# A second fixed order of steps for a pooled-attention and feed-forward kernel, without its twelve filler matmuls

## The chip, the core and the metric

The kernel runs on one core of a Trainium2 chip. The time is device microseconds of one execution; the number compared is the median of the runs of each kernel. TensorE is called PE here, its weight loads PEld, VectorE is DVE, ScalarE is ACT, GpSimd is POOL, and SP issues the DMAs.

## What is computed

Attention over keys and values that are averaged in groups of eight (72 of each are left per head), and behind it a layer norm and a feed-forward block of 512 to 2048 to 512 with a residual, all in float32:

```
k_p = k.reshape(B, H, Sp, pool, D).mean(axis=3)
v_p = v.reshape(B, H, Sp, pool, D).mean(axis=3)
attn = softmax(scale * q @ k_p^T)             # 8 batches x 8 heads, 576 queries, D = 64
x = (attn @ v_p), heads side by side          # 4608 tokens x 512
xn = (x - mu) / np.sqrt(var + 1e-06) * g_ln
out = x + np.maximum(xn @ w_ch1, 0.0) @ w_ch2 # 512 -> 2048 -> 512
```

## The kernel before

Tokens go through in 36 tiles of 128, and the feed-forward block in nine chunks of 512 tokens. Every wide product is made of three f16 matmuls (high times high, low times high, high times low), so each operand has to be split in a high and a low half first; the weights are converted and split on the chip as well.

Each stage is a Python generator whose `yield`s cut it into steps: a step issues instructions to one or two engines. The names that the text uses:

- A.t, the scores of token tile t (eight matmuls, L788; the maximum and subtraction are DVE L798 and L803), and B.t, its values: matmuls L923 to L928, DVE L935 to L956 (row sums, division into tile x, norm statistics), and for the first tiles `parts_turned`, which transposes x on PE with four matmuls into f32 (L876) and one more (L884). B.2 means token tile 2, V.10 is token tile 10 (DVE L982 to L1014).
- C, the conversion of a block of weights (DVE L540); M1 and M2, the maxima that give the scales (ending in a transposition on PE, L467, after DVE L577 to L445); S, the split of a block (ACT L480, DVE L487).
- F.c.f, for chunks 0 and 1, one tile of 128 hidden units of chunk c: twelve matmuls L1111, then ACT L1120 and DVE L1122 out of the PSUM pool ps_f. F.0.f.0 and F.0.f.1 for the first few f are the two halves of the columns.
- G.c.t.h, for chunks 0 to 2, one output tile of 128 tokens and half of the hidden units: 24 matmuls L1314, then DVE L1325 adds to x.
- P.c.h.f.m and O.c.h.n.u, from chunk 2 on, the products of Strassen's scheme in two by two blocks (seven instead of eight): six matmuls L1155 for each product of the first layer, twelve matmuls L1272 for each of the second. ACT L1174 and DVE L1169 and L1172 bring the first ones into a sum in `raw`, DVE L1193 splits them (EL, ER, EP), DVE L1289 adds the second ones to x.
- T, TW: sums of weight blocks that Strassen's scheme needs (T: DVE L615 to L623; TW: DVE L1234 and POOL L1239 to L1247); HK and HV: loads of keys and values and their average (DVE L652, L658; L669); TS.c: a square root by iteration in twelve small DVE instructions (L1029 to L1060); Z and XT: splitting normalised x on POOL and ACT (L1078, L1080) and transposing it by DMA.

What sets the order of the work is written out by hand: two strings of tokens, START (to the end of chunk 1) and STEADY (the rest). Under a manual schedule `run` goes through a string, and each time a token appears it runs the next step of that generator. Every engine so executes its instructions in the order of the strings; semaphores alone decide when.

```
for token in tokens.split():
    if token not in begun:
        name, *args = token.split(".")
        begun[token] = iter(ops[name](*map(int, args)) or ())
    next(begun[token], None)
```

ps_f holds three tiles in START. `KEEP_BUSY = {2: 12}` (L57) makes `parts_turned` issue twelve matmuls of the identity (L872) ahead of its third call (B.2), into the PSUM tile that the transposition then overwrites.

## Time and profile before

| | us |
|---|---|
| runs, shortest, median, longest | 811.84, 813.9, 815.95 |
| the profiled execution, its own time | 814.76 |
| its span in the trace | 813.0 |
| PE busy in the span | 782.8 (96%) |
| DVE busy | 664.0 (82%) |
| ACT, POOL busy | 470.7, 487.6 |

PE is the engine that has least room: 30 us of its span are idle. A span is what lies between the first and the last instruction; 1.8 us lie around it. The median is 0.9 us below the profiled execution.

### The profile page before, as it was taken

The page shows a single profiled execution, that of the slowest core. Times are in us where ns is not written, and L with a number is a line of the kernel's source. Part 1 is how long each engine was busy: PE and PEld are TensorE (multiplying, and loading weights), DVE is VectorE, ACT ScalarE, POOL GpSimd, SP SyncE. Part 2 cuts the span into 40 slices and gives each one's busy share as a digit, 9 for nine tenths or more (in the row PEclk, how much of TensorE's full clock was granted, in tenths as well). Part 3 has the DMA queues.
Part 4 walks back from the last instruction along what each step waited for, and adds up shares of the span by engine and source line. Part 5 has one row for each costly group of instructions (what it writes and reads, how often), then busy time and mean ns, then how long its engine had stood idle before and what let it go on. Part 6 is the DMA issues. An engine that isn't in the chain of part 4 may idle for free.

```text
span 813.0 us, 17388 instructions
## 1 busy us (share of the span) xinstructions
PE 782.8 (96%) x6618; PEld 609.5 (75%) x6618; DVE 664.0 (82%) x1352; ACT 470.7 (58%) x880; POOL 487.6 (60%) x601
## 2 busy tenths in 40 slices
...
DVE  5998999778658999698998998998797868875654
...
GB/s 352 277 151 306 205 188 150 215 8 1 44 120 126 165 217 132 192 188 242 190 174 183 211 192 243 134 250 164 243 85 206 166 134 168 174 152 161 76 120 130
DMA packets 181507, 138.91 MB, mean 171 GB/s; under 512 B 143792, under 2 KB 151600, under 8 KB 179248
## 3 DMA queue, kind: packets, MB, share of 16 engines
...
q14 instruction: 31, 0.25, 0.1%
...
## 4 chain that ended last, share of the span: by engine, by line
PE 54%; DVE 6%; ACT 1%; DMA 1%; issue 1%; DVEq 0%; ACTq 0%
PE ps_f L1155 25%; PE ps_f L1272 25%; PE ps_a L788 2%; PE ps_f L1314 1%; DVE w L1193 1%; DMA ring<-w2s 1%; PE ps_a L927 1%; PE ps_a L928 1%; DVE ring L1185 1%; DVE x L1289 0%; DVE raw L1172 0%; DVE phl L1169 0%; DVE mx L798 0%; DVE raw L1013 0%; DVE raw L1169 0%
## 5 line engine op out<-in xcount | busy, mean ns | idle before, releaser
L1272 PE MATMUL ps_f<-ring,w 128*128 128x256 f16 x2016 | 231.5, 273 | 2.4 <-DVE w L1193 1.0
L1272 PEld LDWEIGHTS <-w 128*128 128x128 f16 x2016 | 196.4, 98 | 26.6 <-DVE w L1193 1.6
L1155 PE MATMUL ps_f<-zts,w 128*128 128x256 f16 x1680 | 206.7, 273 | 2.9 <-DVE raw L1169 1.4
L1155 PEld LDWEIGHTS <-w 128*128 128x128 f16 x1680 | 163.5, 98 | 23.7 <-issue 4.2
L1314 PE MATMUL ps_f<-w,ring 128*128 128x512 f16 x576 | 126.6, 379 | 2.6 <-DVE x L1325 2.2
L1174 ACT COPY raw<-ps_f 128x256 f32<-128x256 f32 x160 | 56.4, 373 | 91.4 <-PE ps_f L1155 80.8
L1314 PEld LDWEIGHTS <-ring 128*128 128x128 f16 x576 | 56.1, 98 | 68.9 <-issue 3.4
L1155 PE MATMUL ps_f<-zts,tsp 128*128 128x256 f16 x672 | 91.0, 273 | 1.7 <-ACT raw L1174 1.7
L1111 PE MATMUL ps_f<-zts,w 128*128 128x512 f16 (+1 forms) x480 | 86.9, 338 | 1.5 <-DVE w L487 1.4
L1191 ACT CAST w<-w 128x512 f16<-128x512 f32 x96 | 58.9, 618 | 44.6 <-POOL w L1211 24.5
L1193 POOL TENSOR_TENSOR w<-w 128x512 f16<-128x512 f32 x48 | 58.3, 1214 | 32.2 <-ACT w L1191 24.4
L1111 PEld LDWEIGHTS <-w 128*128 128x128 f16 x480 | 46.3, 98 | 37.8 <-DVE w L487 1.9
L1155 PEld LDWEIGHTS <-tsp 128*128 128x128 f16 x672 | 65.0, 98 | 10.1 <-issue 2.2
L1210 POOL TENSOR_TENSOR w<-raw 128x256 f32<-128x256 f32 x32 | 25.0, 780 | 65.5 <-ACT raw L1202 37.9
L1289 DVE SCALAR_TENSOR_TENSOR x<-ps_f,y,x 128x256 f32<-128x256 f32 (+1 forms) x84 | 42.0, 517 | 24.2 <-PE ps_f L1272 23.1
L824 POOL TENSOR_TENSOR phl<-e,phl 128x512 f16<-128x512 f32 x32 | 39.0, 1220 | 37.5 <-ACT phl L814 37.5
L1080 POOL TENSOR_TENSOR hl<-raw,hl 128x640 f16<-128x640 f32 x28 | 40.9, 1463 | 25.9 <-ACT hl L1078 25.8
L1289 DVE SCALAR_TENSOR_TENSOR x<-ps_f,cy,x 128x256 f32<-128x256 f32 (+1 forms) x84 | 42.2, 516 | 14.1 <-PE ps_f L1272 13.6
L1193 DVE TENSOR_TENSOR w<-raw,w 128x512 f16<-128x512 f32 (+1 forms) x64 | 45.0, 709 | 3.9 <-ACT w L1191 3.9
L788 PE MATMUL ps_a<-kblk,q 128*128 128x144 f32 (+1 forms) x320 | 43.3, 294 | 3.7 <-issue 2.5
L1169 DVE TENSOR_TENSOR raw<-ps_f,raw 128x256 f32<-128x256 f32 x80 | 32.2, 415 | 15.9 <-ACT raw L1174 9.4
L1120 ACT ACTIVATE ring<-ps_f 128x512 f16<-128x512 f32 (+1 forms) x40 | 19.4, 506 | 43.9 <-PE ps_f L1111 29.6
...
## 6 DMA issues: line engine op xcount, KB each, us to landing
...
```

The source lines that it names most:

```text
L788: nc.tensor.matmul(ps[r, p // 2, p % 2 * 2 * KV : (p % 2 + 1) * 2 * KV], lhsT=q[:, p, r], rhs=kblk[b % NKB][:, p, :], start=True, stop=True,)
L824: nc.gpsimd.tensor_tensor(out=ph[:, 0, :, KA:P], in0=e[:, :, 0:KA], in1=ph[:, 0, :, 0:KA], op=ALU.subtract)
L1080: nc.gpsimd.tensor_tensor(out=zhl[:, 1, :], in0=src, in1=zhl[:, 0, :], op=ALU.subtract)
L1111: nc.tensor.matmul(ps, lhsT=w[:, part, fs], rhs=zT[:, kz, cols], start=(n == 0), stop=(n == 3 * NKT - 1),)
L1155: nc.tensor.matmul(ps, lhsT=w[:, part, f * P : (f + 1) * P], rhs=z, start=m in (1, 2, 4, 5) and n == 0, stop=m in (2, 3, 4, 7) and n == 3 ...
L1169: nc.vector.tensor_tensor(out=o, in0=ps, in1=o, op=ALU.add)
L1174: nc.scalar.copy(out=o, in_=ps)
L1191: nc.scalar.copy(out=hi, in_=src)
L1193: engine.tensor_tensor(out=lo, in0=src, in1=hi, op=ALU.subtract)
L1272: nc.tensor.matmul(ps, lhsT=wt[2][:, left, part, f * HC + u * P : f * HC + (u + 1) * P], rhs=b[:, f // FPB, wp, f % FPB], start=n < 4 and ...
L1289: nc.vector.scalar_tensor_tensor(out=x, in0=ps, scalar=scale, in1=x, op0=ALU.mult, op1=ALU.add)
L1314: nc.tensor.matmul(ps, lhsT=h[:, part, i, cols], rhs=w[:, wp, j], start=(n == 0), stop=(n == 3 * NFT // 2 - 1),)
```

## The change

Both strings are replaced. They hold the same work, in another order on every engine, and the filler matmuls with their counter are gone (24 rows of PE, twelve matmuls and twelve weight loads). The numbers of lines fall by 2 below the strings and by 9 below `parts_turned`: L876 is L867 after, L1111 is L1102, L1325 is L1316, L1193 is L1184.

```
-KEEP_BUSY = {2: 12}
...
 START = """
-LN.2 LN.2 LK.0 LK.0 LK.1 LK.1 Q.0 Q.0 R.1.0 R.1.0 R.1.1 R.1.1 Q.1 Q.1 R.1.2 R.1.2 R.1.3 R.1.3 A.0 HV.1.0 LG LG R.2.0
...
+LN.2 LN.2 LK.0 LK.0 LK.1 LK.1 Q.0 Q.0 LG LG R.1.0 R.1.0 R.1.1 R.1.1 Q.1 Q.1 R.1.2 R.1.2 R.1.3 R.1.3 A.0 HK.1.0 HV.1.0
...
 STEADY = """
-P.2.0.0.2 P.2.0.0.1 P.2.0.0.5 P.2.0.1.2 P.2.0.0.1 P.2.0.0.1 P.2.0.0.6 P.2.0.1.1 P.2.0.1.1 P.2.0.1.1 P.2.0.0.5 P.2.0.0.5
...
-    n_turned = [0]
-
     def parts_turned(x, ln, cv, dst):
         ps = psum["ps_m"].tile([P, CH], F32, name="ps_m").rearrange("p (k c) -> p k c", k=NKT)
-        n_turned[0] += 1
-        for _ in range(KEEP_BUSY.get(n_turned[0] - 1, 0)):
-            nc.tensor.matmul(
-                ps, lhsT=ident, rhs=ident.unsqueeze(1).broadcast_to([P, NKT, P]), start=True, stop=True
-            )
         for k in range(NKT):
```

Three places of the new order are shown. The first is PE just ahead of the transposition of token tile 2 (x). Before, the last two of the twelve fillers (`ident`) stand there:

```order
L872 LDWEIGHTS ident
L872 MATMUL ps_m<-ident 128x512
L876 MATMUL ps_m<-zts,x 128x128 x4
L884 MATMUL ps_m<-zts,ln 128x512
L923 LDWEIGHTS pt
```

After, the last of 36 matmuls of the first layer stand there (F.0.0.0, F.0.1.0 and F.0.2.0, w_90 being the split weights):

```order
L1102 LDWEIGHTS w_90
L1102 MATMUL ps_f<-zts,w_90 128x256
L867 MATMUL ps_m<-zts,x 128x128 x4
L875 MATMUL ps_m<-zts,ln 128x512
L914 LDWEIGHTS pt
```

These 36 stood behind that transposition, and behind the values of tile 3, before.

The second place is DVE at the start of the second half of the first layer of chunk 1 (F.1.8 and on; L1325 is the last addition of G.1.3.0, L1122 takes a tile out of ps_f; raw is a weight sum of T or a normalised tile of V.10, kr keys, or TW where it comes from w_91). Before:

```order
L1325 SCALAR_TENSOR_TENSOR x<-ps_f,cy,x 128x512
L623 TENSOR_TENSOR raw<-raw 128x512
L935 TENSOR_SCALAR sm<-ps_a,cv 128x8
L943 RECIPROCAL rs<-sm 128x8
L945 TENSOR_TENSOR x<-ps_a,rs 128x512
L955 BN_STATS st<-x 128x6
L956 BN_AGGR ln<-st 128x2
L982 TENSOR_SCALAR z<-x,ln 128x512
L1122 SCALAR_TENSOR_TENSOR ring<-ps_f,ring 128x512 x5
L982 TENSOR_SCALAR raw<-x,ln 128x512
L1007 TENSOR_SCALAR raw<-x,ln 128x512
```

After:

```order
L1316 SCALAR_TENSOR_TENSOR x<-ps_f,cy,x 128x512
L621 TENSOR_TENSOR raw<-raw 128x512
L1113 SCALAR_TENSOR_TENSOR ring<-ps_f,ring 128x512
L650 TENSOR_REDUCE kr<-kr 128x72
L656 COPY kblk_114<-kr 64x72 x2
L973 TENSOR_SCALAR raw<-x,ln 128x512
L998 TENSOR_SCALAR raw<-x,ln 128x512
L1225 TENSOR_TENSOR kr<-w_91 128x256 x2
L1002 TENSOR_TENSOR raw<-raw 128x256
L1003 TENSOR_TENSOR raw<-raw 128x256
L1004 TENSOR_TENSOR raw<-raw 128x256
L1005 TENSOR_TENSOR raw<-raw 128x256
```

Before, five ps_f tiles (F.1.8 to F.1.12) were taken out in a row, and the average of keys, V.10 and TW.0.0.0 came later. After, those stand between the first tile and the second.

The third place is DVE between the last sums of the second half of chunk 3's first layer and the second layer that reads them (L1193 writes the split factors w_91, L1169 and L1172 the sums in raw, L1029 and L1032 open TS.4, L976 is a small step of token tile 19). Before:

```order
L1193 TENSOR_TENSOR w_91<-phl_116,w_91 128x256
L669 TENSOR_REDUCE vp<-vr 72x64
L1169 TENSOR_TENSOR raw<-ps_f,raw 128x256 x2
L1193 TENSOR_TENSOR w_91<-w_91 128x2x256
L1172 TENSOR_TENSOR raw<-ps_f,raw 128x2x256
L976 TENSOR_SCALAR ln<-ln 128x1
L1193 TENSOR_TENSOR w_91<-raw,w_91 128x2x256 x2
```

After:

```order
L667 TENSOR_REDUCE vp<-vr 72x64
L1160 TENSOR_TENSOR raw<-ps_f,raw 128x256
L1020 TENSOR_SCALAR ve<-ln 128x4
L1023 TENSOR_SCALAR y<-ve 128x4
L1184 TENSOR_TENSOR w_91<-w_91 128x2x256
L1163 TENSOR_TENSOR raw<-ps_f,raw 128x2x256
L1184 TENSOR_TENSOR w_91<-raw,w_91 128x2x256
L967 TENSOR_SCALAR ln<-ln 128x1
L1184 TENSOR_TENSOR w_91<-phl_116,w_91 128x256
L1184 TENSOR_TENSOR w_91<-raw,w_91 128x2x256
```

The split `w_91<-phl_116` (ER.3.1.1) has moved behind the sum L1172, and TS.4 has come in ahead; the splits EL.3.1.2 and EL.3.1.3 are the rows `w_91<-raw` in both.

On PE around G.2 (chunk 2's second layer, groups of 24 matmuls L1314 among groups of six matmuls L1155) the order after the scores of tile 17 was, before: G.2.0.1, two products, G.2.3.1, two products, G.2.2.1. After: G.2.3.1, G.2.0.1, one product, G.2.2.1, the values of tile 16, one product, G.2.1.1.

## Rows read from the trace of the kernel before

**Rows 1.** The page: the span, busy time of each engine, and the busy tenths of DVE in 40 slices of 20.3 us (9 is 90% or more).

```profile
span 813.0 us, 17388 instructions
PE 782.8 (96%) x6618; PEld 609.5 (75%) x6618; DVE 664.0 (82%) x1352; ACT 470.7 (58%) x880; POOL 487.6 (60%) x601
...
DVE  5998999778658999698998998998797868875654
```

**Rows 2.** Windows of the span: stretch, length, then busy us (and instructions) of each engine, the granted clock as a share of full speed, the DMA share and GB/s.

```profile
100.00:120.00 20.00, 17.38 (x93) 9.27 (x92) 19.38 (x30) 16.96 (x25) 17.23 (x22) 0.91 0.79 195
...
112.00:114.00 2.00, 2.00 (x9) 1.65 (x9) 2.00 (x2) 2.00 (x4) 1.92 (x2) 0.50 0.72 183
...
380.00:400.00 20.00, 20.00 (x196) 18.06 (x195) 18.15 (x36) 16.02 (x33) 12.71 (x13) 1.00 0.77 168
```

**Rows 3.** The waits of PE over the whole span: line, what it waited for, us in total, times, the longest.

```profile
PE ps_m L728 <- DMA w<-in_kvn_dram: 6.8, 1, 6.8
...
PE ps_f L1155 <- DVE raw L1169: 1.4, 2, 0.8
...
PE ps_f L1272 <- DVE w L1193: 1.0, 2, 0.8
```

**Rows 4.** The timeline of PE and, below, of DVE around the fillers: start, length (of the group), engine, line, operation, count, and in brackets the idle time before it and what ended it.

```profile
42.84 2.75 PE L872 MATMUL ps_m<-ident 128*128 128x512 bf16 x12 [0.63 <-ACT z L897]
...
46.82 1.16 PE L876 MATMUL ps_m<-zts,x 128*128 128x128 f32 x8 [1.23 <-DVE x L945]
...
49.45 4.09 PE L1111 MATMUL ps_f<-zts,w 128*128 128x256 f16 x36
...
46.07 0.69 DVE L945 TENSOR_TENSOR x<-ps_a,rs 128x512 f32<-128x512 f32 x1
...
47.63 1.45 DVE L487 SCALAR_TENSOR_TENSOR w<-w,gs 128x1024 f16<-128x1024 f32 x1
```

**Rows 5.** The timeline of PE from 104 to 120 us, where the clock was halved; the last row is DVE's.

```profile
109.96 0.39 PE L1111 MATMUL ps_f<-zts,w 128*128 128x512 f16 x1 [1.44 <-DVE w L487]
...
111.53 2.26 PE L788 MATMUL ps_a<-kblk,q 128*128 128x144 f32 x8 [1.18 <-issue]
...
113.58 3.21 PE L1111 MATMUL ps_f<-zts,w 128*128 128x512 f16 x12
...
117.15 2.75 PE L1111 MATMUL ps_f<-zts,w 128*128 128x512 f16 x12
...
119.74 0.22 PE L467 MATMUL ps_m<-ident,rowmax 128*128 128x128 bf16 x1
...
117.74 0.15 DVE L445 TENSOR_SCALAR rowmax<-rowmax 128x1 int32<-128x1 int32 x1
```

**Rows 6.** The timeline of DVE from 199 to 225 us, the steps that the second place above moves.

```profile
200.90 1.63 DVE L623 TENSOR_TENSOR raw<-raw 128x512 f32<-128x512 f32 x1 [0.72 <-POOL raw L621]
...
207.22 0.69 DVE L1122 SCALAR_TENSOR_TENSOR ring<-ps_f,ring 128x512 f16<-128x512 f32 x1 [1.62 <-ACT ring L1120]
...
212.80 0.54 DVE L982 TENSOR_SCALAR raw<-x,ln 128x512 f32<-128x512 f32 x1
...
213.71 0.42 DVE L1011 TENSOR_TENSOR raw<-raw 128x256 f32<-128x256 f32 x1
...
220.57 0.74 DVE L652 TENSOR_REDUCE kr<-kr 128x72 f32<-128x576 f32 x1
...
221.34 1.05 DVE L658 COPY kblk<-kr 64x72 f32<-64x72 f32 x2
...
222.43 2.83 DVE L1234 TENSOR_TENSOR kr<-w 128x256 f32<-128x256 f16 x2
```

**Rows 7.** The timeline of PE from 255 to 327 us, the groups that waited; the last row is DVE's.

```profile
256.71 0.49 PE L1155 MATMUL ps_f<-zts,tsp 128*128 128x256 f16 x3 [1.08 <-ACT raw L1174]
...
277.55 0.81 PE L1155 MATMUL ps_f<-zts,w 128*128 128x256 f16 x6 [0.58 <-DVE raw L1169]
...
301.91 1.47 PE L1155 MATMUL ps_f<-zts,w 128*128 128x256 f16 x12 [0.37 <-DVE x L1325]
...
304.64 0.81 PE L1155 MATMUL ps_f<-zts,tsp 128*128 128x256 f16 x6 [0.61 <-ACT raw L1174]
...
310.53 1.22 PE L788 MATMUL ps_a<-kblk,q 128*128 128x144 f32 x8 [0.81 <-PE ps_f L1155]
...
326.95 5.34 PE L1314 MATMUL ps_f<-w,ring 128*128 128x512 f16 x24 [2.23 <-DVE x L1325]
...
326.15 0.75 DVE L1325 SCALAR_TENSOR_TENSOR x<-ps_f,cy,x 128x512 f32<-128x512 f32 x1
```

**Rows 8.** The timeline of DVE, and in the last row of PE, from 391 to 401 us, and the opening of TS.4 where it stood.

```profile
391.53 1.09 DVE L1193 TENSOR_TENSOR w<-phl,w 128x256 f16<-128x256 f32 x1
...
393.81 0.67 DVE L1193 TENSOR_TENSOR w<-w 128x512 f16<-128x512 f32 x1
394.40 0.68 DVE L1172 TENSOR_TENSOR raw<-ps_f,raw 128x512 f32<-128x512 f32 x1
...
395.13 1.53 DVE L1193 TENSOR_TENSOR w<-raw,w 128x512 f16<-128x512 f32 x2
...
409.40 0.95 DVE L1029 TENSOR_SCALAR ve<-ln 128x4 f32<-128x4 f32 x1
...
395.74 5.40 PE L1272 MATMUL ps_f<-ring,w 128*128 128x256 f16 x48
```

More of the change, by code (lines that the diff above doesn't have):

```diff
@@ new lines @@
+B.12 P.2.1.1.5 P.2.1.1.5 P.2.1.0.5 P.2.1.0.5 P.2.1.1.6 P.2.1.0.6 P.2.1.0.3 P.2.1.1.3 P.2.1.1.6 P.2.1.1.6 P.2.1.0.6
+P.2.1.0.6 TW.0.2.1 B.13 P.2.1.0.2 P.2.1.0.2 P.2.1.0.4 TW.0.3.0 B.13 TW.0.3.0 TW.0.3.0 P.2.1.0.3 P.2.1.0.3 P.2.1.1.2
+A.15 HV.4.1 HV.4.1 HK.4.0 TW.0.2.1 TW.0.2.1 P.2.1.1.3 P.2.1.1.3 TW.0.3.0 P.2.1.1.2 P.2.1.1.2 P.2.1.1.4 P.2.1.0.7
+P.2.1.1.7 B.12 HV.4.1 HV.4.1 A.15 B.14 G.2.0.0 A.15 P.2.1.0.4 P.2.1.0.4 B.13 HK.4.0 HK.4.0 A.16 TW.0.3.0 TW.0.3.0
+HK.4.1 KW.1.0 KW.1.0 HV.5.0 B.14 HV.4.1 A.15 A.15 A.15 KW.0.1 KW.0.1 B.14 B.14 P.2.1.1.4 P.2.1.1.4 B.13 P.2.1.0.7
@@ new lines @@
+ES.3.0.0 ES.3.0.0 P.3.0.3.1 P.3.0.3.1 P.3.0.3.6 ER.3.0.0 ER.3.0.0 P.3.0.3.5 P.3.0.3.5 EP.3.0.0.1 EP.3.0.0.0 P.3.0.2.1
+P.3.0.2.1 P.3.0.3.3 TW.1.3.1 TW.1.3.1 TW.1.3.1 HV.5.1 LW.3.0.0 LW.3.0.0 A.19 LW.3.0.1 LW.3.0.1 G.2.2.1 G.2.2.1
+P.3.0.1.3 P.3.0.1.3 P.3.0.2.5 EL.3.0.1 P.3.0.3.6 P.3.0.3.6 B.16 P.3.0.3.2 P.3.0.3.2 P.3.0.3.4 P.3.0.3.4 P.3.0.3.4
+EP.3.0.0.1 EP.3.0.0.1 A.18 B.17 P.3.0.2.6 P.3.0.2.2 P.3.0.2.2 P.3.0.2.4 P.3.0.3.7 EP.3.0.0.0 EP.3.0.0.0 P.3.0.3.3
+P.3.0.3.3 P.3.1.0.2 EL.3.0.3 P.3.0.2.4 P.3.0.2.4 P.3.0.2.5 P.3.0.2.5 P.3.0.2.6 P.3.0.2.6 A.18 P.3.0.2.3 P.3.1.0.1
@@ new lines @@
+O.5.1.0.0 O.5.1.0.0 EP.5.1.2.1 EP.5.1.2.1 O.5.1.0.1 O.5.1.0.1 O.5.1.1.1 O.5.1.1.1 O.5.1.2.1 O.5.1.1.0 O.5.1.1.0
+ES.5.1.3 ES.5.1.3 EP.5.1.3.1 O.5.1.3.0 O.5.1.3.0 B.27 B.27 Z.27.0 Z.27.1 TS.6 O.5.1.2.1 O.5.1.2.1 TS.6 Z.27.0 Z.27.0
+EP.5.1.3.1 EP.5.1.3.1 HK.7.0 HK.7.0 LW.5.1.5 LW.5.1.5 LW.5.1.4 LW.5.1.4 A.29 A.29 O.5.1.2.0 O.5.1.4.0 P.6.0.0.1
+O.5.1.5.0 O.5.1.4.1 P.6.0.0.1 P.6.0.0.1 LW.5.1.6 LW.5.1.6 XT.27.0 XT.27.0 HK.7.1 O.5.1.2.0 O.5.1.2.0 Z.27.1 Z.27.1
+XT.27.1 XT.27.1 O.5.1.3.1 O.5.1.3.1 O.5.1.5.1 O.5.1.4.1 O.5.1.4.1 O.5.1.6.1 A.28 A.28 A.28 O.5.1.4.0 O.5.1.4.0
@@ new lines @@
+P.6.1.3.5 P.6.1.2.2 B.30 B.30 Z.30.0 Z.30.1 O.6.0.5.1 O.6.0.5.1 P.6.1.3.1 P.6.1.2.5 O.6.0.5.0 P.6.1.2.5 P.6.1.2.5
+P.6.1.3.1 P.6.1.3.1 EP.6.1.0.0 EP.6.1.0.0 ER.6.1.0 ER.6.1.0 P.6.1.2.2 P.6.1.2.2 P.6.1.2.4 B.31 P.6.1.2.3 P.6.1.2.6
+P.6.1.2.4 P.6.1.2.4 EP.6.1.0.1 P.6.1.3.5 P.6.1.3.5 P.6.1.2.6 P.6.1.2.6 ES.6.1.1 EP.6.1.1.0 EL.6.1.1 EL.6.1.1 Z.30.1
+Z.30.1 O.6.0.5.0 O.6.0.5.0 P.6.1.3.2 P.6.1.3.6 P.6.1.2.7 P.6.1.3.3 P.6.1.3.6 P.6.1.3.6 XT.30.1 XT.30.1 LW.6.1.2
+LW.6.1.2 P.6.1.3.7 EP.6.1.0.1 EP.6.1.0.1 B.31 P.6.1.2.3 P.6.1.2.3 EL.6.1.2 ES.6.1.1 ES.6.1.1 P.6.1.3.2 P.6.1.3.2
```

586 lines of the change are left out of this document (283 added, 303 removed).

## The prediction

> **What bounds the kernel now.** I read the page first: PE is busy for 782.8 of 813.0 us [rows 1], so 30.2 us of its time are idle, and no order of the same work can take more than that away. The first 6.8 us of it wait for a load [rows 3] that the change leaves where it is, and another part is the tail behind PE's last matmul, whose tokens are nearly the same. Some 20 us are left, and the question is which engine ends them. The windows answer that for the first 120 us: DVE is at nine tenths or more in most of these slices [rows 1], and from 100 to 120 it works 19.38 of 20 us while PE works 17.38 [rows 2]. DVE is the bound there, and PE's waits are what DVE's queue leaves. Later PE runs through whole windows without a gap (20.00 of 20 from 380 to 400), with DVE close behind at 18.15 [rows 2]. So only a place where DVE now finishes earlier, or where PE has more to do before it asks DVE, can gain; and where DVE gets more to do ahead of a result, new waits can come.
>
> **The change, part by part.** The sum is made on the profiled execution (span 813.0, time 814.76) and then taken off the median of the runs, 813.9.
>
> 1. *The fillers.* They took 2.75 us, and yet PE waited 1.23 us more behind them, for L945 of token tile 2, which ended at 46.07 + 0.69 = 46.76; PE went on at 46.82 [rows 4]. They lie inside one wait for DVE, so their removal gives 0 in itself. The 36 matmuls of F.0.0.0 to F.0.2.0 that move into this wait took 4.09 us [rows 4]; that would be a gain if they could run there. They can't: the fourth block of rows of the weights that each of these tiles needs is split by the L487 that began at 47.63 and ended at 49.08, and PE's group began at 49.45, right behind it [rows 4]. By the order that L487 comes about one small group of DVE earlier (the row sum, division and statistics of tile 2 now stand behind it, a conversion ahead), some 0.8 us. Then the transposition of tile 2 (1.16 us and its last matmul) lies behind the 36, so its followers are later by about what the others gain. I take 0, with -1 and +1 as bounds (a gain of what DVE comes earlier, or a loss of the transposition's 1.16).
>
> 2. *The rest of the first 120 us.* The maximum of the second weight matrix ends in the transposition L467, which PE reached at 119.74, behind a group of twelve L1111 [rows 5]. Its last DVE step, L445, had ended at 117.74 + 0.15 = 117.89 [rows 5]. In the new order the DVE steps of the maximum come ahead of one L1122 (0.69 us, [rows 6]) and L467 comes ahead of that group, so PE has it at about 117.2, 2.5 us earlier; against that the scores A.10 (eight L788, 1.0 us of PE's time without the fill of the pipe, 1.22 with it [rows 7]) are still to be done then. What is gained is 2.5 - 1.0: **-1.5**. Bounds: -0.5 if DVE is held up elsewhere (it has 0.6 us of free time in this window [rows 2]), -2.5 if A.10 costs nothing because it fills a wait.
>
> 3. *A new wait at F.1.12.* ps_f has three tiles, so F.1.12 can begin when DVE has taken F.1.9 out. After, between the last L1325 and that L1122 stand: L623 1.63, the L1122 of F.1.8, then L652 0.74, L658 1.05, two normalisations 2 x 0.54, TW's L1234 2.83, four L1011 to L1014 at 0.42, and L1122 0.69 [rows 6]. F.1.8 itself ends 2.59 us after its start on PE (twelve at 2.75 with the fill of the pipe, [rows 5]), and ACT stands between, so DVE begins the first L1122 at about 3.3 us; behind it 0.69 + 0.74 + 1.05 + 1.08 + 2.83 + 1.68 + 0.69 = 8.76 us follow, so F.1.9's tile is free at 12.1. PE reaches F.1.12 after four groups, 4 x 2.59 = 10.4. The wait is 1.7; I take **+1.5**, bounds 0 (DVE may be ahead by then; POOL's sums may let L623 run early) and 2.5 (L623 waited 0.72 for POOL, [rows 6]). Before, five L1122 stood in a row there and PE did not wait.
>
> 4. *240 to 327 us.* The waits were 1.08 + 0.58 + 0.37 + 0.61 + 0.81 + 2.23 = 5.7 us [rows 7]. The largest is for L1325 of G.2.0.1, which ended at 326.90, while PE had run two groups of 24 and four products (a group is 5.34 with the fill of the pipe, 5.18 in a row; 12 matmuls of the products take 1.47, 1.31 in a row: 2 x 5.18 + 4 x 0.65 = 13.0, with the scores A.17 14.0) since the last result of DVE that it needed [rows 7]. In the new order PE has the scores A.17, three groups of 24 and a product ahead of the next such point, the values of tile 16 (1.0 + 3 x 5.18 + 0.65 = 17.2 us), 3.2 us more cover than before against a wait of 2.23. So 2.23 goes. What is late next is the drain of product sums by ACT and DVE, the five smaller waits, together 3.45: a new order can keep or lose each, and I take a little under half, 1.57, as gone. **-3.8**; bounds -5.7 (all) and -1.5 (the new order keeps them all and a part of the large one, because DVE is itself the bound here and arrives no earlier).
>
> 5. *Chunk 3, second half, about 395 us.* In the new order DVE has, from the sum that PE's last products wait on to the last split factor: TS.4's opening, 0.95 and a small row, L1193 0.67, L1172 0.68, L1193 0.77 (half of 1.53), the moved L1193 1.09, and L1193 0.77 [rows 8], 4.9 us, with the small rows some 5.2. PE meanwhile has two products (1.3), the scores A.20 (1.0) and three quarters of a group of twelve (5.40/4 = 1.35 with the fill, 1.0) [rows 8]: 3.3. The difference is a wait of 1.9 us at the first O. Before, the moved split began at 391.53, three us earlier, and TS.4 stood at 409.40 [rows 8]. Against it stand the waits of the later chunks that the old order had, 1.0 for L1193 and 0.8 for L1169 [rows 3], of which I take nearly all, 1.6, as gone. **+0.3**, bounds -1.8 (no new wait) and +2.5 (the old ones stay in part).
>
> The sum is 0 - 1.5 + 1.5 - 3.8 + 0.3 = **-3.5 us**: a span of 809.5, a profiled time of 811.3, and against the median of the runs **810.4 us**.
>
> **Rivals.** *The clock.* In the window from 112 to 114 PE ran at 0.50 of its clock (1.2 of 2.4 GHz) after waits of 1.44 and 1.18 us; the eight L788 took 2.26 us instead of 1.22, the twelve L1111 3.21 instead of 2.75 [rows 2, 5, 7], together +1.5, with the matmul ahead of them some 1.7. The fillers kept PE at work where now it only waits, 42 to 47 us; if the clock falls there, the 36 matmuls behind run at half speed for a while. With +1.7, and DVE as the bound hiding none of it, the time is 810.4 + 1.7 = 812.1. For it speaks that the fall at 111 came after two waits shorter in sum than this one; against it that nine of the 36 moved matmuls, whose weights are there, run inside the wait. The Trainium skill has the rule behind this rival (TensorE: Matmul & The Clock Gate, "What's actually happening"): the throttled state is the default, and activity releases it; the trace agrees in that the half clock follows the waits.
>
> *Given back.* DVE works over 19 of 20 us in much of the first 330 us (nines in most slices, [rows 1]). If term 2 and term 4 only move waits, because DVE comes to the same L1325 at the same time, the gain shrinks to the 0.5 of term 2 and the 1.5 of term 4, less the 1.5 of term 3: 813.4.
>
> *Slower.* The pattern of term 5, splits moved just ahead of their reader, may repeat in each half of the later chunks; DVE is at 18.15 of 20 in such a stretch [rows 2], and each wait costs 1.9. There are ten such halves behind it. To end slower by 0.5% (4.1 us), the later ones must eat the 3.5 and 4.1 more, which is four of them (7.6); five cost 9.5 and give 819.9. Against it: in the later slices DVE is at 6 to 8 tenths [rows 1], which leaves cover.
>
> *Larger gain.* If all waits of term 4 go and term 3 finds DVE ahead: -1.5 - 5.7 + 0.3 = -6.9, 807.0.
>
> **How the numbers follow.** A measurement of this kernel tells about 0.5% from no change (the runs lie within 0.25% of their median), so faster means below 809.8. The sum's own case has a chance of 0.53, with a range of 807.5 to 813.5 from its bounds, half of it below 809.8 (0.26); larger gain 0.14, faster; the clock 0.08 and given back 0.10, both the same; slower 0.15. Faster 0.40, same 0.45, slower 0.15. The range leaves out about 0.07 of the larger gain below and 0.11 of the slower case above: 805.5 to 816.5.
>
> **What would show it.** Term 1: the PE row behind the 36 L1102 begins within 1 us of 54. Term 2: the last transposition of the maximum (L465 after) near 117. Term 3: an idle time of some 1.5 us before an L1102 near 205 to 210, put down to DVE L1113. Term 4: no idle time over 1 us before an L1305 around 325. Term 5: a wait of about 2 us before the first L1263 near 395, put down to DVE L1184. The clock: a granted clock under 0.9 in the windows 40 to 50 or 110 to 120. The prediction is wrong if PE's idle time within the late windows, where it is nothing now, grows by more than 4 us.

## The result and the profile after

The change makes the kernel slower: 820.9 us (median; 820.65 to 822.5) against 814.1 us (811.84 to 815.95) for the kernel before (813.9 in the three runs on record with the prediction), four runs each, a ratio of 1.0087 with a 95% interval of 1.0061 to 1.0112. The profiled execution took 822.5 us. The forecast was 810.4 us, with a range of 805.5 to 816.5; the result lies outside it, on the side of the rival called *slower*.

The page after, with the lines that answer to [rows 1]: the span, the busy times, and the busy tenths of DVE in 40 slices of 20.5 us.

```profile
span 820.7 us, 17336 instructions
PE 783.4 (95%) x6606; PEld 609.7 (74%) x6606; DVE 664.9 (81%) x1352; ACT 471.2 (57%) x880; POOL 489.3 (60%) x601
...
DVE  5999998788528999798988898988887768785664
```

Every engine does the same work as before to within 2 us. The span has grown by 7.7 us and PE's idle time from 30.2 to 37.3 us, 7.1 of them. So the kernel is not slower because of something that it does, but because PE waits more. The waits of PE over the whole span, as in [rows 3] (line, what it waited for, us in total, times, the longest), say for what:

```profile
PE ps_m L726 <- DMA w<-in_kvn_dram: 6.6, 1, 6.6
PE ps_f L1146 <- DVE raw L1160: 4.8, 4, 1.6
PE ps_a L918 <- DVE e L801: 3.1, 2, 2.6
PE ps_f L852 <- DVE mx L796: 3.0, 3, 2.2
...
PE ps_f L1102 <- DVE w L485: 1.5, 1, 1.5
...
PE ps_f L1263 <- DVE w L1184: 1.5, 3, 0.8
```

The load at the start stays what it was. The wait of Strassen's first-layer products for the addition L1160 (L1169 before) is 4.8 us where it was 1.4, and most of the rest is DVE too: all that PE waited for DVE comes to 22.4 us, where it was 11.4. Where the waits lie is seen by windows of the two kernels over the same stretch, chunks 2 to 4 (busy us and instructions of PE, PEld, DVE, ACT and POOL, granted clock, DMA share, GB/s). Before:

```profile
310.00:500.00 190.00, 185.68 (x1700) 157.33 (x1701) 166.04 (x355) 116.46 (x233) 123.16 (x153) 1.00 0.77 196
```

After:

```profile
310.00:500.00 190.00, 177.96 (x1613) 148.18 (x1612) 168.45 (x339) 114.77 (x229) 132.03 (x163) 1.00 0.72 184
```

In 190 us PE does 7.7 us less, at full clock throughout. DVE is busy for 2.4 us longer and yet gets through 16 instructions fewer; POOL is busy for 8.9 us longer. This row is the centre of the case.

PE's places, in order of time (start, length of the group, engine, line, operation, count, idle time before it and what ended it; the groups at 211.07 and 402.32 are longer, their rows end with the window that was asked for):

```profile
29.69 0.70 PE L852 MATMUL ps_f<-zts,mx 128*72 128x128 f32 x2 [2.19 <-DVE mx L796]
...
48.69 2.90 PE L1102 MATMUL ps_f<-zts,w 128*128 128x256 f16 x25 [1.51 <-DVE w L485]
52.48 1.16 PE L867 MATMUL ps_m<-zts,x 128*128 128x128 f32 x8 [0.89 <-DVE x L936]
...
84.67 2.26 PE L786 MATMUL ps_a<-kblk,q 128*128 128x144 f32 x8 [1.34 <-issue]
...
118.77 0.23 PE L465 MATMUL ps_m<-ident,rowmax 128*128 128x128 bf16 x1 [0.36 <-DVE rowmax L443]
...
199.93 10.52 PE L1102 MATMUL ps_f<-zts,w 128*128 128x512 f16 x48 [0.36 <-DVE x L1316]
211.07 4.26 PE L1102 MATMUL ps_f<-zts,w 128*128 128x512 f16 x19 [0.63 <-DVE ring L1113]
...
331.58 0.19 PE L918 MATMUL ps_a<-va,pt 128*128 128x65 f16 x1 [2.60 <-DVE e L801]
...
344.22 1.47 PE L1146 MATMUL ps_f<-zts,w 128*128 128x256 f16 x12 [0.91 <-DVE raw L1160]
...
352.62 0.49 PE L1146 MATMUL ps_f<-zts,tsp 128*128 128x256 f16 x3 [1.37 <-ACT raw L1165]
...
395.57 0.81 PE L1146 MATMUL ps_f<-zts,tsp 128*128 128x256 f16 x6 [1.56 <-DVE raw L1160]
...
402.32 0.94 PE L1263 MATMUL ps_f<-ring,w 128*128 128x256 f16 x7 [0.48 <-DVE w L1184]
```

How late the new kernel is against the old, taken where PE has done the same amount of work in both traces: about 3 us at 31 us, 4.4 at 93, -0.1 at 113, 2.4 at 247, -0.1 at 308, -2.0 at 327, 0.7 at 336, 4.0 at 351, 5.5 at 402, 8.0 at 452, 9.9 at 533, and 7.7 at the end. (The orders differ, so such a number is good to some tenths.) Two things are to be seen in this list. Up to 327 us delays come and go, and the new order has lost nothing by then. From 308 to 533 us it loses 10 us in small pieces, none above 2.6, and little comes back.

### The profile page after: what moved, and what is told of

It is laid out like the page before. It is cut to its first block, busy times and chain, and to the rows that moved or that the text cites. A ratio compares the mean times of both kernels' runs of the same rounds, so it can differ in the third digit from the quotient of the medians.

```text
span 820.7 us, 17336 instructions
## 1 busy us (share of the span) xinstructions
PE 783.4 (95%) x6606; PEld 609.7 (74%) x6606; DVE 664.9 (81%) x1352; ACT 471.2 (57%) x880; POOL 489.3 (60%) x601
## 4 chain that ended last, share of the span: by engine, by line
PE 48%; DVE 7%; POOL 1%; issue 1%; ACT 0%; DVEq 0%; POOLq 0%
PE ps_f L1263 24%; PE ps_f L1146 21%; DVE w L1184 2%; PE ps_a L786 1%; DVE x L1280 1%; PE ps_a L918 1%; PE ps_a L919 1%; DVE raw L1160 0%; DVE kblk L656 0%; DVE mx L796 0%; POOL hl L1071 0%; DVE raw L1163 0%; DVE e L801 0%; DVE st L946 0%; DVE x L936 0%
## 5 line engine op out<-in xcount | busy, mean ns | idle before, releaser
L1146 PE MATMUL ps_f<-zts,w 128*128 128x256 f16 x1680 | 207.4, 273 | 1.9 <-DVE raw L1160 0.9
L1146 PEld LDWEIGHTS <-w 128*128 128x128 f16 x1680 | 163.3, 98 | 22.2 <-issue 2.8
L1146 PE MATMUL ps_f<-zts,tsp 128*128 128x256 f16 x672 | 91.8, 272 | 5.8 <-DVE raw L1160 3.9
L1102 PE MATMUL ps_f<-zts,w 128*128 128x512 f16 (+1 forms) x480 | 86.4, 336 | 5.3 <-DVE ring L1113 2.9
L1184 POOL TENSOR_TENSOR w<-w 128x512 f16<-128x512 f32 x48 | 59.9, 1248 | 37.1 <-ACT w L1182 36.9
L1102 PEld LDWEIGHTS <-w 128*128 128x128 f16 x480 | 46.2, 98 | 41.9 <-issue 6.0
L1146 PEld LDWEIGHTS <-tsp 128*128 128x128 f16 x672 | 65.2, 98 | 14.7 <-issue 7.0
L822 POOL TENSOR_TENSOR phl<-e,phl 128x512 f16<-128x512 f32 x32 | 39.6, 1239 | 42.6 <-ACT phl L812 29.3
L1071 POOL TENSOR_TENSOR hl<-raw,hl 128x640 f16<-128x640 f32 x28 | 39.8, 1427 | 30.2 <-ACT hl L1069 27.1
L1184 DVE TENSOR_TENSOR w<-raw,w 128x512 f16<-128x512 f32 (+1 forms) x64 | 45.0, 710 | 4.7 <-ACT w L1182 4.5
L1111 ACT ACTIVATE ring<-ps_f 128x512 f16<-128x512 f32 (+1 forms) x40 | 19.8, 507 | 41.7 <-PE ps_f L1102 41.7
L1184 DVE TENSOR_TENSOR w<-w 128x512 f16<-128x512 f32 x48 | 39.5, 822 | 4.0 <-ACT w L1182 3.9
```

The lines of the kernel that those rows point to most:

```text
L822: nc.gpsimd.tensor_tensor(out=ph[:, 0, :, KA:P], in0=e[:, :, 0:KA], in1=ph[:, 0, :, 0:KA], op=ALU.subtract)
L1071: nc.gpsimd.tensor_tensor(out=zhl[:, 1, :], in0=src, in1=zhl[:, 0, :], op=ALU.subtract)
L1102: nc.tensor.matmul(ps, lhsT=w[:, part, fs], rhs=zT[:, kz, cols], start=(n == 0), stop=(n == 3 * NKT - 1),)
L1146: nc.tensor.matmul(ps, lhsT=w[:, part, f * P : (f + 1) * P], rhs=z, start=m in (1, 2, 4, 5) and n == 0, stop=m in (2, 3, 4, 7) and n == 3 ...
L1184: engine.tensor_tensor(out=lo, in0=src, in1=hi, op=ALU.subtract)
```

## The experiments

In the tables of numbers here, *START time* is the start of chunk 2's first product in the profile (240.80 us before, 243.16 after), and *STEADY time* what passes from there to PE's last matmul (568.9 before, 574.3 after). STEADY time repeats well: in the four profiled executions with the whole new STEADY and its edits in START alone it is 574.3 to 574.7. START time is looser. PE's first products begin at 14.1 to 16.1 us, by the execution, and falls of the clock come in some executions only: of eight with the old START three ran for 3.4 us at half clock from about 111 us, the kernel before among them [rows 5]; of six with the new START and no fillers five did so from 82 to 84 us, and two from about 29.6, the changed kernel in both. Ratios are against the kernel before in runs on the same chip.

### Which part of the change does it

**The old order without fillers.**

```
-KEEP_BUSY = {2: 12}
+KEEP_BUSY = {}
```

> The old order of both strings, without the twelve filler matmuls. Theory of waits (the loss comes from steps that DVE now has ahead of results PE asks for; the fillers lay inside a wait for DVE): the same as before within 0.3%, since PE was released at 46.82 by DVE's L945 of token tile 2 and not by the fillers. Theory of the clock (without fillers the granted clock falls and what follows is late): slower by 2 to 4 us, with a granted clock under 0.9 in the window 40 to 50.

Measured: 815.9 against 813.2, ratio 1.0031 (1.0013 to 1.0049), some 2.6 us slower. PE's timeline at the gap:

```profile
45.72 2.04 PE L876 MATMUL ps_m<-zts,x 128*128 128x128 f32 x8 [4.68 <-ACT w L480]
```

The windows there (columns as above):

```profile
44.00:46.00 2.00, 0.28 (x1) 0.31 (x2) 1.90 (x5) 1.49 (x2) 1.84 (x4) 0.64 1.01 426
46.00:48.00 2.00, 2.00 (x9) 1.89 (x9) 1.97 (x4) 2.00 (x3) 1.92 (x3) 0.50 0.31 87
```

The transposition that stood behind the fillers begins at 45.72 instead of 46.82 [rows 4]. The whole trace is ahead there by nearly as much (the group of the same line before it begins at 38.32 instead of 39.50), so the transposition is some 0.1 us late and no wait becomes longer by the fillers' loss. But the waits before, between and behind them are now one of 4.68 us, and the granted clock falls to 0.50 (1.2 of 2.4 GHz) and stays there for some 6.8 us: the transposition takes 2.04 us instead of 1.16. By the next transposition (61.68 us against 60.43) the lead of 1.2 us has become 1.2 us of delay. The fillers are worth some 2.6 us, and the trace shows no other cause for it than the clock.

**One string at a time.** The new START without fillers before the old STEADY; then the old START with its fillers before the new STEADY.

```
-KEEP_BUSY = {2: 12}
+KEEP_BUSY = {}
...
 START = """
+(START of the changed kernel)
```

> The new START (no fillers) with the old STEADY. At equal work of PE the new kernel is 2.4 us behind the old one where STEADY begins (P.2 at 243.2 against 240.8). Theory of waits that add up by place: +2 to +2.5 us, about 816.4. If DVE as the bound of the next stretch takes a delay of PE back, or if the clock falls of the first 100 us are all of it: 0 to +1.

Measured: 815.8, ratio 1.0032 (1.0018 to 1.0047), 2.6 us slower; START time 241.6, STEADY time 569.5.

```
 STEADY = """
+(STEADY of the changed kernel)
```

> The old START with its fillers and the new STEADY. Theory of waits that add up by place: +5.3 us, about 819.4, which with the run of the new START sums to the whole difference. If the new STEADY is only late because it begins late with other transfers and sums still under way: under +2.

Measured: 820.1, ratio 1.0079 (1.005 to 1.0107), 6.4 us slower; START time 239.4, STEADY time 574.7, and the clock full up to PE's last matmul. Both orders are worse, STEADY by more than twice. By their ratios the parts, 2.6 and 6.4, come to 9.0 us, where the whole is 7.1: they don't quite add.

**The changed kernel with the fillers back** (both strings new, `KEEP_BUSY = {2: 12}` kept).

> The new order of both strings with the twelve fillers put back ahead of the transposition of token tile 2. Theory of waits: the new kernel's own time within 2 us, if anything slower, since the fillers now stand behind 36 matmuls and in a shorter wait (0.9 us before the transposition). Theory of the clock: faster than the new kernel by 3 us or more.

Measured: 822.4, ratio 1.0106 (1.0081 to 1.013), not better than the changed kernel. The half clock lies at 29.2 and 83.9 us in it, as at 29.7 and 84.3 in the changed kernel; neither is near the fillers. The new order has matmuls of its own in that wait, the 36 and, from 42.62 us, eight pairs of the small L845 and L852, and the clock stays whole from 40 to 50 us without fillers. Which of them it takes was not tried.

### START

**The keys of the second load later.** The 2.19 us wait at 29.69 comes from the averaging of keys HK.1.0 (DVE 26.80 to 28.84 us) that the new order has ahead of token tile 2's maximum (28.88 to 29.64; before 26.44 to 27.19). This kernel moves its two steps behind the next block's conversion.

```
 M1.0
-HK.1.0
-HK.1.0
 E.1.1
...
 C.2.0
+HK.1.0
+HK.1.0
 C.1.3
```

> The new kernel with one step in START moved: the average of keys HK.1.0 (L650 and L656 on DVE, 2 us) stands behind the maximum of the scores of tile 2 again. In the new kernel it stood ahead of it, PE waited 2.18 us at 27.5 and its clock was at half from 29.7 to 33.1. Theory of places: the wait and the half clock go, and the first P of STEADY comes 2 to 4 us earlier. Theory of the bound: the wait and the half clock go too, but DVE, the bound of the first 110 us, takes it back: the first P of STEADY is earlier by under 0.7 us and the time falls by less than that.

Measured: 821.6, ratio 1.0097 (1.0071 to 1.0123), no gain. The waits of PE (timeline):

```profile
27.80 0.44 PE L852 MATMUL ps_f<-zts,mx 128*72 128x128 f32 x2 [0.57 <-DVE mx L796]
38.50 0.44 PE L852 MATMUL ps_f<-zts,mx 128*72 128x128 f32 x2 [3.44 <-DVE mx L796]
42.06 2.05 PE L867 MATMUL ps_m<-zts,x 128*128 128x128 f32 x8 [1.32 <-ACT w L478]
```

The wait of 2.19 is 0.57, and 3.44 and 1.32 stand some ten microseconds later, with a half clock behind them (39.6 to 46.4 us). DVE's work is the same and is due all the time there; taking it from one wait puts it into the next. The delay of 4.4 us at 93 us that is gone at 113 has two sources. Some 2.6 us are waits that the old order has there, 1.44 for DVE's L487 and 1.18, [rows 5], and that a late PE no longer meets: waits behind one late DVE don't add. Some 1.5 are the half clock behind them [rows 5], which only some executions of the old START have.

### STEADY: single waits

**POOL's sums ahead of the split.** The largest wait of the new trace, 2.60 us at 331.58, has a chain that can be read. The rows of DVE, then of POOL, of the changed kernel:

```profile
323.20 2.90 DVE L1225 TENSOR_TENSOR kr<-w 128x256 f32<-128x256 f16 x2 [1.46 <-POOL phl L1238]
326.02 1.35 DVE L1033 TENSOR_TENSOR a<-y 128x4 f32<-128x4 f32 x1
...
330.68 0.76 DVE L801 TENSOR_TENSOR e<-ps_a,mx 128x576 f32<-128x576 f32 x1
...
310.15 2.76 POOL L1071 TENSOR_TENSOR hl<-raw,hl 128x640 f16<-128x640 f32 x2
...
322.01 2.27 POOL L1238 TENSOR_TENSOR phl<-kr,phl 128x512 f16<-128x512 f32 x2
324.24 3.12 POOL L1071 TENSOR_TENSOR hl<-raw,hl 128x640 f16<-128x640 f32 x2
```

PE waits for A.17's exponent input, L801, which ends at 331.44. Ahead of it DVE had waited 1.46 us for POOL's split L1238 of a weight sum, and POOL was late with that because Z (L1071) now stands ahead of the sums. Then two L1225 took 2.90 us instead of 0.75, and a square-root step on 128x4 took 1.35 us instead of 0.15, each while POOL was inside a long subtraction. The edit moves the sums TW.1.0.1 ahead of Z.

```
 TW.1.0.0
+TW.1.0.1
+TW.1.0.1
 A.16
 A.16
+TW.1.0.1
+TW.1.0.1
 P.2.1.3.7
...
 TW.1.1.0
-TW.1.0.1
-TW.1.0.1
-TW.1.0.1
 A.16
 TW.1.1.0
 TW.1.1.0
-TW.1.0.1
```

> The new kernel with one weight sum moved: TW.1.0.1's steps on POOL and ACT stand ahead of the two splittings Z.14 on POOL again, as in the old order, where they ended 13 us earlier. In the new kernel DVE waited 1.46 us at 321.7 for the last of them, came to the scores of tile 17 at 329.9, and PE waited 2.59 us at 329.0 for that. Theory of places (a delay of one step is passed on by the queue behind it and costs PE what it waits): both waits go, -2 to -3 us, about 818. Theory of a bound (DVE has so much to do from 260 to 350 us that PE waits for it anyway, a little later): -0.5 or less, with a longer wait at 340 to 352.

Measured: 821.7, ratio 1.0099 (1.0073 to 1.0124). PE's waits from 305 to 335 us (timeline; numbers of lines are 2 lower than after's):

```profile
310.74 1.22 PE L784 MATMUL ps_a<-kblk,q 128*128 128x144 f32 x8 [1.79 <-issue]
317.32 5.57 PE L1303 MATMUL ps_f<-w,ring 128*128 128x512 f16 x25 [0.40 <-DVE ring L1174]
330.35 0.19 PE L916 MATMUL ps_a<-va,pt 128*128 128x65 f16 x1 [1.62 <-DVE e L799]
```

The wait falls from 2.60 to 1.62; that at 310 grows from 0.88 to 1.79, and one of 0.40 is new: 3.81 us against 3.48. The cause was read rightly, and taking it away gains nothing.

**The additions first.** The waits of L1146 for L1160 at 394, 446 and 483 us have one form: a later product adds into the same PSUM tile that DVE must have read out first, and in the new order DVE has keys, values or square-root steps (HK.5.0, HK.6.0, TS.4) ahead of that addition. The edit puts the additions ahead, at four places of this kind:

```
 P.3.1.2.6
+P.3.1.2.2
+P.3.1.2.2
+P.3.1.3.2
+P.3.1.3.2
 HK.5.0
...
+P.4.1.0.2
+P.4.1.0.2
 TS.4
...
+P.4.1.3.2
+P.4.1.3.2
 HK.6.0
```

> The new kernel with four additions of DVE (L1160: P.3.1.2.2, P.3.1.3.2, P.4.1.0.2, P.4.1.3.2) put ahead of averages of keys and values and of TS.4, behind which they stood. PE's fourth products wait for just these additions: 1.56 us at 394.0, 1.39 at 446.3, 0.94 at 482.6. Theory of places: the three waits go, -3 to -3.9 us, about 817.3. Theory of the bound: each wait comes back at the first second-layer group behind it (401 to 402, 449 to 457, 494), and the time falls by 1 us or less.

Measured: 820.6, ratio 1.0087 (1.0058 to 1.0116), the same as the changed kernel. Its waits of PE (lines 2 lower than after's):

```profile
PE ps_f L1261 <- DVE w L1182: 4.0, 6, 1.2
...
PE ps_f L1144 <- DVE raw L1158: 0.9, 1, 0.9
```

The waits for the additions fell from 4.8 to 0.9 us, and those of the second layer for the split factors grew from 1.5 to 4.0. That fits a DVE that is behind as a whole and not by its order at one place.

### STEADY: where the loss needs the new order

Three kernels follow one order up to a token and then take the rest of the work in the sequence of the other.

**Old to the end of chunk 4 (about 500 us), new behind it.**

```
 STEADY = """
-(all tokens behind O.4.1.5.1, old order)
+(the same tokens, new order)
```

> The old kernel, fillers included, up to the last second-layer group of chunk 4 (some 500 us), and from there on the new order. Behind 500 us the new kernel's PE waits 0.4 us in all, the old one's some 1.9. Theory of places: -1 to -1.7 us against before, about 812.5. If the new order is free of waits there only because its PE was held back earlier and DVE had a lead: the same as before within 0.3, with waits of 0.5 us or more behind 500.

Measured: 813.1, ratio 0.9994 (0.9981 to 1.0008). The new order behind 500 us costs nothing.

**Old to A.17's first step (about 310 us), new behind it.**

```
 STEADY = """
-(all tokens behind the first step of A.17, old order)
+(the same tokens, new order)
```

> The old START, fillers and STEADY up to the scores of tile 17 (about 311 us), and from there on the new order. Theory of collisions (behind 310 us DVE is the bound, and in the new order its instructions begin more often while POOL is in one of its own and take about a microsecond longer: from 300 to 500 us 24 against 14 that took over 0.5 us more than their kind, 19.8 us more against 10.1): the loss sits behind 310, so +4 to +6 us against before. Theory of lost idle time (from 220 to 260 us DVE idled 22 us in the new order and 11 in the old one, so it comes late to all that follows): the loss sits ahead of 310, so 0 to +1.5.

Measured: 817.2, ratio 1.0035 (1.0018 to 1.0052); STEADY time 572.4, 3.5 longer than before's.

**New to A.17's first step, old behind it.** The expectation speaks of the new START; the kernel that ran has the old START with its fillers, so it tests STEADY alone.

```
 STEADY = """
-(all tokens to the first step of A.17, old order)
+(the same tokens, new order)
```

> The new START without fillers and the new STEADY up to the scores of tile 17, and from there on the old order. Theory of collisions: the new START's +2.6 and no more, less up to 2 us that the new order gains from 240 to 310, so 0 to +3 against before. Theory of lost idle time: as the new kernel, +5 to +7.

Measured: 814.2, ratio 0.9999 (0.9986 to 1.0012); STEADY time 568.4. So the part ahead of 310 us costs nothing by itself, and the part behind it costs 3.5 of the 5.4 by itself. The other 2 appear only when both are new.

**New to 310 us, old to 500, new again** (old START).

```
 STEADY = """
-(old order)
+(new to A.17's first step, old to O.4.1.5.1, then new)
```

> The old START with its fillers; STEADY in the new order up to the scores of tile 17 (310 us), in the old one from there to the end of chunk 4 (500 us), and in the new one behind it. Theory of places kept where they cost nothing: the two gains seen apart (0.5 us of STEADY for the first part, 1.0 for the last) add up, -0.5 to -1.5 us against before. If each part's gain hangs on what stands ahead of it: 0, within 0.3 us.

Measured: 815.9, ratio 1.0013 (0.9998 to 1.0027); STEADY time 570.2, with 6.8 us at half clock from 326.7 us in it. With the middle old, most of the loss is gone; the loss sits between 310 and 500 us.

### DVE and POOL

In that stretch I counted the DVE instructions that last over 0.5 us longer than the lower quartile of their own line and shape. From 300 to 500 us there are 23 in the changed kernel (19.2 us over) and 14 in the one before (9.8 us; the expectations count without the shapes, 24 with 19.8 and 14 with 10.1), and each of them began while a POOL instruction was under way, or within 0.3 us of its start. A place at 480 us of the changed kernel (DVE, then POOL) shows which kinds:

```profile
479.81 0.75 DVE L650 TENSOR_REDUCE kr<-kr 128x72 f32<-128x576 f32 x1
480.59 2.42 DVE L656 COPY kblk<-kr 64x72 f32<-64x72 f32 x2
...
479.25 1.23 POOL L1205 TENSOR_TENSOR w<-raw 128x256 f32<-128x256 f32 x1
480.44 1.39 POOL L1071 TENSOR_TENSOR hl<-raw,hl 128x640 f16<-128x640 f32 x1
481.80 1.15 POOL L1184 TENSOR_TENSOR w<-w 128x512 f16<-128x512 f32 x1
```

The reduction under L1205 takes its usual 0.75 us. The two copies, 0.2 us each elsewhere, take 1.30 and 1.10: each ends about when the POOL instruction does that was running as it began (481.83, 482.95). Over the whole trace the additions L1160 and L1163, which read one operand from PSUM, and the reductions L667 and L796 never last longer under POOL than alone (at most 0.43, 0.69, 0.68 and 0.76 us). The Trainium skill (SBUF — State Buffer, "Who interferes with whom") states it: copies, casts and tensor_scalar can, and a DVE instruction with two inputs in SBUF does, against a POOL instruction that reads SBUF, contend for a shared pair of ports, which one instruction holds for its whole length while the other fully blocks; a reduction on trn2 never contends. This trace agrees, kind by kind, and for two inputs mostly. Of the instructions of the changed kernel that began inside a POOL subtraction or addition with more than their usual time (by 0.1 us) of it left, all 18 copies and 53 of 65 with two inputs in SBUF lasted to its end, and none of 12 reductions and of 103 with an operand in PSUM. Why 12 of the 65 did not is not shown.

**POOL relieved, in both orders.** ACT copies where POOL subtracted for Z, and the low halves of the pair sums and of the later tiles' probabilities are worked out for a few columns only, so these two leave out a part of the low halves. DVE keeps all its work.

```
-        nc.gpsimd.tensor_tensor(out=zhl[:, 1, :], in0=src, in1=zhl[:, 0, :], op=ALU.subtract)
+        nc.scalar.copy(out=zhl[:, 1, :], in_=src)
...
+        if engine is nc.gpsimd:
+            lo, src, hi = lo[:, :, :16], src[:, :, :16], hi[:, :, :16]
...
+        n = KA if t < 3 * TPC else 4
...
-            out=ph[:, 0, :, KA:P], in0=e[:, :, 0:KA], in1=ph[:, 0, :, 0:KA], op=ALU.subtract
+            out=ph[:, 0, :, KA:KA + n], in0=e[:, :, 0:n], in1=ph[:, 0, :, 0:n], op=ALU.subtract
```

The new order so relieved:

> The new order with POOL relieved: the low halves of z are not computed but copied by ACT, and POOL's subtractions for the low halves of the pair sums (from chunk 3 on) and of the probabilities (from tile 12 on) do 16 columns, or 4, of each. So POOL has some 130 us less to do, and the low halves are wrong. Theory of collisions: DVE's instructions over 0.5 us longer than their kind become few in both orders, the new order loses most of its excess, and the two orders with a relieved POOL differ by under 3 us instead of 6.9. If the order's own waits are the cause: the difference stays at 5 us or more.

Measured: 809.8, ratio 0.9955 (0.9939 to 0.997); POOL busy 353 us instead of 489, STEADY time 561.8. The old order so relieved:

> The old order with the same relief of POOL, to be compared with the new order so relieved. Theory of collisions: it gains little itself, 0 to 3 us against before, and stands under 3 us from the other. If the order's own waits are the cause: the other is 5 us or more slower.

Measured: 806.7, ratio 0.9912 (0.9893 to 0.9931); POOL busy 356 us, STEADY time 562.4. The window of 310 to 500 us of the new order so relieved:

```profile
310.00:500.00 190.00, 189.21 (x1746) 160.18 (x1745) 160.12 (x365) 127.48 (x254) 86.16 (x149) 1.00 0.80 199
```

And of the old order so relieved:

```profile
310.00:500.00 190.00, 188.88 (x1759) 161.32 (x1758) 159.99 (x360) 125.44 (x253) 79.88 (x140) 1.00 0.78 200
```

PE is at 189 of 190 us in both. The 7.7 us between the orders in this stretch are gone, and the STEADY times agree within 0.6 us; what is left between the kernels, 3.1 us, is START's. With POOL out of the way the new STEADY is as good as the old. The stretched instructions fall to 5 in each (3.1 us).

**POOL's long subtractions in two halves, in both orders.** The same work in instructions of half the columns: a DVE instruction that is blocked should then wait half as long.

```
-        nc.gpsimd.tensor_tensor(out=zhl[:, 1, :], in0=src, in1=zhl[:, 0, :], op=ALU.subtract)
+        for j in range(2):
+            cols = slice(j * n * P // 2, (j + 1) * n * P // 2)
+            nc.gpsimd.tensor_tensor(out=zhl[:, 1, cols], in0=src[:, cols], in1=zhl[:, 0, cols], op=ALU.subtract)
```

(and the same for the subtractions at L822, L1184 and L1238). The new order:

> The new kernel with POOL's four longest subtractions of STEADY (low halves of z, of the pair sums, of the probabilities and of TW) each done in two instructions of half the columns: the same work and the same order. Theory of collisions (DVE waits until the POOL instruction under way has ended): what DVE loses to one falls to half, some 5 of the 20 us between 300 and 500 at the places where these four are met, and PE gets 1.5 to 3 us of it back: about 818.5. If it is POOL's results that DVE and ACT wait for, and not its instructions under way: POOL has more instructions to start, so no change or up to 2 us slower.

Measured: 819.4, ratio 1.0064 (1.0043 to 1.0085); STEADY time 572.0. DVE and POOL of it at one place (L1035 to L1042 are after's L1033 to L1040, L1075 is L1071):

```profile
323.99 0.75 DVE L1035 TENSOR_TENSOR a<-y 128x4 f32<-128x4 f32 x1
324.77 0.71 DVE L1036 TENSOR_TENSOR a<-a,ve 128x4 f32<-128x4 f32 x1
325.52 0.71 DVE L1037 SCALAR_TENSOR_TENSOR y<-a,y 128x4 f32<-128x4 f32 x1
326.27 0.72 DVE L1042 TENSOR_TENSOR y<-y,ln 128x4 f32<-128x4 f32 x1
...
323.75 3.21 POOL L1075 TENSOR_TENSOR hl<-raw,hl 128x320 f16<-128x320 f32 x4
```

Four small instructions, four halves of 0.80 us: each lasts until its half ends. Against whole instructions the wait of one is halved, and now four of them wait, where two did. The old order so halved:

> The old kernel with the same halving. Theory of collisions: it has half as many collisions from 300 to 500, so it gains 0 to 1.5 us. If POOL's results are what counts: no change or up to 2 us slower.

Measured: 809.8, ratio 0.9944 (0.9923 to 0.9965), span 808.7; STEADY time 565.6. This computes everything that the kernel before does and is faster than both kernels, 4.6 us than before and about 11 than after. What the stretched instructions take from 300 to 500 us falls from 19.2 to 8.8 us (new) and from 9.8 to 6.0 (old), and the STEADY times by 2.3 and 3.3 us. The difference between the orders does not shrink with it: it was 5.4 us and is 6.5. The 572.0 of the new order holds 3.4 us at half clock from 329.9 us, which cost some 1.2 (six L1150 took 1.47 us instead of 0.82, a group of 24 5.90 instead of 5.34); without it the difference is about 5.3, as large as before.

So two things are shown, and one is open. Blocking by POOL costs time in both orders: POOL's shorter instructions gained in both, although they gave POOL more to do (515 and 517 us busy instead of 489 and 488). The new order's loss in STEADY needs POOL's load. But that the larger number of blocked instructions is the loss is not shown: with the halves the surplus of blocked time between the orders fell from 9.4 to 2.8 us, and the loss stayed.

The other half of POOL's effect is that DVE and ACT wait for its results. DVE's wait for POOL's split L1238 is no candidate: in this stretch it is 4.8 us after and 3.3 before, and in the relieved kernels, where the loss is gone, still 4.3 and 3.1. ACT's waits are one. The largest, after, then before:

```profile
ACT w L1182 <- POOL w L1202: 16.5, 5, 5.8
...
ACT w L1191 <- POOL w L1211: 6.0, 6, 1.8
```

In sum ACT waits for POOL from 310 to 500 us for 36.3 us after and 20.6 before; with halves for 40.6 and 24.5; relieved for 17.2 and 11.9. The surplus of the new order, 15.7, 16.1 and 5.3 us, goes with the loss where the blocked time does not. That is no proof: DVE itself waits for ACT there for 5.4 us against 4.4, and PE for 1.8 against none, so the way from ACT's waits to all of the loss is not seen; an engine also waits longer when all is late; and the relieved kernels give DVE more free time than either order has (627 and 638 us busy instead of 665), which hides small differences of any kind. No run takes ACT's waits away alone.

## Why the prediction was wrong

**What bounds the kernel.** The reading of the first 120 us held in the main: DVE is the bound there, and waits that were taken away came back (the kernel with the keys later). The "nines in most slices" of the first 330 us were too many: [rows 1] has a nine in 8 of 16. The reading of what comes later was too kind. That PE "runs through whole windows without a gap", "with DVE close behind at 18.15" [rows 2], was taken as cover; it was a balance with 1.85 us to spare in 20, and the new order uses it up.

**What no term covered: the first 45 us.** The keys' average HK.1.0 stands ahead of token tile 2's maximum in the new START, and the sum has nothing for it. PE waited the 2.19 us at 29.69 for it and, in this execution, ran at half clock for 3.4 us behind it; it was 4.1 us late at the scores (35.39 against 31.30) and 2.9 at the first of the 36 matmuls (45.09 against 42.21, where the wait for the fillers began, [rows 4]).

**Term 1, the fillers: 0.** Nearly right in sum for the new order, not in its reasoning. The 36 matmuls began at 45.09 us, and the wait for the split of the fourth block showed (1.51 us, L485), but eleven ran ahead of it, where the prediction had nine. The transposition stands at 52.48, 1.5 us ahead of the 54 that it was to be within 1 of. PE was 2.9 us late where the wait began and 1.7 at the next scores (55.20 against 53.48), so this place gave 1.2 back, a little more than the bound of -1. That removing the fillers "gives 0 in itself" was false: in the old order it costs some 2.6 us. The argument looked only at when the next result comes, not at the clock.

**Term 2, the maximum: -1.5.** L465 came at 118.77 instead of 119.74: 1.0 us earlier instead of 2.5. PE, 1.7 us late at 55, was 1.0 late at 134. The bound of -0.5, "if DVE is held up elsewhere", was the nearer one.

**Term 3, F.1.12: +1.5.** Right: waits of 0.36 and 0.63 at the place named, the second put down to the line named, and 1.3 us of delay over 199 to 214.

**Term 4, 240 to 327 us: -3.8.** This is the first step that failed. The local part was right: from 247 to 308 us the new order gained 2.5, the wait at G.2.0.1 of 2.23 [rows 7] is gone, as the cover of 17.2 us said, and at 327 us, where the term ends, 4.4 us were gained. But 5 us later the wait of 2.60 at 331.58 took most of it, and 0.47, 0.91 and 1.37 up to 352.62 the rest and more. The step counted a wait as gone where it had moved: it reckoned PE's work ahead of the next result and left DVE's durations as they stood in the old trace; that DVE "arrives no earlier" was only a bound, and no term stood for what PE would wait for next. DVE came later, because POOL's sums stood behind Z and because DVE's instructions met POOL's. By 351 us the term was +1.6 where -3.8 was forecast, 5.4 us off.

**Term 5, chunk 3: +0.3.** The second failed step, 5.6 us off. The wait of 1.9 at the first O did come, in another place: 1.56 us at a product of the first layer (395.57) and 0.48 at O (402.32). What was wrong is the credit of -1.6 for the waits of the later chunks, "of which I take nearly all, 1.6, as gone". They grew. From 351 to 533 us the new order lost 5.9 us; behind it 2.2 came back, for which the sum had nothing. Together the places give the whole miss of 11.2 us, from -3.5 to +7.7: 2.9 for the first 45 us, -1.2, 0.8, -0.2, 5.4 and 5.6 for the five terms, and -2.2 behind them (11.1).

**The rivals.** *Slower* had the right sign and the right stretch: short waits behind DVE in several halves of the chunks, priced at 819.9 us, measured 820.9. That the number fits is luck. Its mechanism, the split L1184 ahead of its reader, cost PE 1.5 us in all where it was 1.0; it was mostly the addition L1160 and A.17's subtraction L801, and some 2.6 us of the loss are START's, which the rival did not have. What spoke against it, DVE at 6 to 8 tenths in the later slices, was true and did not help, since the loss lay in slices mostly at 8 and 9. *The clock* fell, twice (29.7 to 33.1 and 84.3 to 87.7 us, behind waits of 2.19 and of 0.48 and 1.34), but not where the fillers had been; it was worked out for 42 to 47 us, where PE now had real work. The fall at 111 us that stood in the old trace is not in the new one. *Given back* had the mechanism of term 4, a wait that moves, and stopped near 0 where the sum went on to a loss.

**The test that was named.** PE's idle time in the late windows was to stay within 4 us. It grew by 7.7 us from 310 to 500 us alone.
